# Attention, then a gated FFN, on one core: the kernel rewritten with hand-ordered engines

## The chip, the cores and the metric

One core of a Trainium2 chip runs the whole kernel. The metric is the device time of one execution in microseconds (us). Executions are called fast or slow by their time and by the clock that was granted to TensorE (PE below); ratios use fast ones only. DVE is VectorE, ACT is ScalarE, POOL is GpSimd, SP is SyncE, and PEld is TensorE's loading of weights. A line number such as L185 is a line of the profiled kernel. Numbers of before and of after are those of different programs, so the same line number means different things in them.

## The reference

Eight batches of 576 tokens, eight heads of 64. The attention is linear ("cosformer"): there is no softmax, only features, two small products and a division. Then comes a feed-forward network with a GELU gate, 512 to 1536 to 512, over all 4,608 tokens. All inputs and the output are fp32.

```python
def phi(x, c, s):                       # 64 -> 128 features
    r = np.maximum(x, 0.0)
    return np.concatenate([r * c, r * s], axis=-1)
q_p, k_p = phi(q, cos_w, sin_w), phi(k, cos_w, sin_w)
kv  = einsum('bhsf,bhsd->bhfd', k_p, v)
z   = sum(k_p, axis=2)
num = einsum('bhsf,bhfd->bhsd', q_p, kv)
den = einsum('bhsf,bhf->bhs', q_p, z)[..., None] + 1e-06
x   = (num / den), as tokens x 512
out = (gelu(x @ w_gate) * (x @ w_val)) @ w_out
```

In counts of 128x128x512 products, the FFN has 432 each for the gate, the value and the output. (The traces count 480 matmuls for the gate and 480 for the value, because some are narrower than 512.) That is nearly all the work of TensorE. The attention's products are small, but its transposes, scalings and loads are many.

## The kernel before

A scheduler orders the engines. The attention of a batch runs, then as many FFN chunks of 512 tokens as the finished batches allow. The parts that matter here:

```python
ffn_psum = ctx.enter_context(tc.tile_pool(name="ffn_psum", bufs=1, ...))   # one bank each: g_ps, v_ps, o_ps
def ffn_chunk(t0, n):
    for jt in range(JT):                       # 12 gate/value units
        g_ps = ...; for ct in range(CT): nc.tensor.matmul(g_ps[:, 0:n], lhsT=wg_sb[...], rhs=xT_sb[...])
        v_ps = ...; for ct in range(CT): nc.tensor.matmul(v_ps[:, 0:n], lhsT=wv_sb[...], rhs=xT_sb[...])
        nc.scalar.activation(gel[:, 0:n], g_ps[:, 0:n], AF.Gelu)
        nc.vector.tensor_mul(hT[:, jt, 0:n], gel[:, 0:n], v_ps[:, 0:n])
    ...                                        # o_ps: 12 matmuls per 128 tokens, copy, store
# loads: 256-byte rows, cast to bf16 on the GpSimd queue, one transfer per tile of 128 tokens
nc.gpsimd.dma_start(out=qk_sb[:L, 1], in_=q[b, :, ss:ss + L, :].transpose([1, 0, 2]))
# both transposes of the attention on TensorE, copied out by DVE and ACT
nc.tensor.transpose(out=qpt_ps[:, h, 0:L], in_=kqp[:L, 1, h, :], identity=ident[:L, :L])
nc.tensor.transpose(out=xt_view[:, 0:L], in_=attn_bt[:L, 4 * g:4 * g + 2, :], identity=ident[:L, :L])
```

## Time and profile before

Three runs before the prediction had a median of 412.06 us.

| | before |
|---|---|
| median of 3 runs | 412.06 us (410.91 to 413.91) |
| PE busy | 365.0 us, 89% of 411.5 us |
| one gate/value unit in the steady part | 1.87 us |
| one output tile (12 matmuls) | 2.59 us |
| last wo_sb in SBUF, its wait on the chain | 27.46 us |

From the page of the kernel before: busy time, two rows of the 40 slices (tenths busy; PEclk is the granted clock in tenths), the packets, and the chain of waits that ended last.

```profile
PE 365.0 (89%) x2467; PEld 192.7 (47%) x2512; DVE 181.0 (44%) x416; ACT 121.7 (30%) x256; POOL 102.8 (25%) x163
...
PE   0032899999999999999999999999999999999995
...
PEclk9999989999999999999999999999999999999999
...
DMA packets 121390, 29.90 MB, mean 73 GB/s; under 512 B 113168, under 2 KB 115728, under 8 KB 121360
...
PE 78%; DMA 10%; POOL 5%; DVE 3%; issue 2%; ACT 1%; DVEq 0%; POOLq 0%
PE v_ps L90 23%; PE o_ps L103 23%; PE g_ps L81 21%; DMA wo_sb<-in_moe_w_out_dram 7%; PE kv_ps L187 4%; PE qpt_ps L174 3%; DMA qk_sb<-in_k_dram 2%; DMA qk_sb<-in_q_dram 2%; PE nmA L203 2%; PE nmB L203 1%; DVE hT L99 1%; POOL qk_sb L129 1%; P
```

TensorE is full from the sixth slice on; the first four are nearly empty. So there are two parts: a start that waits for loads, and a long stretch in which only less TensorE time helps. Nearly all packets are under 512 bytes.

The timeline of TensorE in a stretch that holds FFN units only (start, duration, instruction, count; in other lines a bracket gives the idle time before the instruction and what ended it, where "issue" means nothing that the profile shows):

```profile
157.14 1.02 PE L90 MATMUL v_ps<-xT_sb,wv_sb 128*128 128x512 bf16 x4
158.00 1.03 PE L81 MATMUL g_ps<-xT_sb,wg_sb 128*128 128x512 bf16 x3
159.01 1.02 PE L90 MATMUL v_ps<-xT_sb,wv_sb 128*128 128x512 bf16 x4
```

The value products begin at 157.14 and 159.01: a unit takes 1.87 us. From value to gate it is 0.86 us, from gate to value 1.01 us. At 0.216 us for a matmul (2.59 / 12) eight would take 1.73 us. The timeline of weight loads has the missing 0.14 us: before each value group its second load waits 0.27 us. What it waits for the view of waits does not name ("issue"), but DVE's product of the unit before, which reads the one bank of v_ps, ends at 158.96 us, and the group begins at 159.01.

```profile
159.01 0.53 PEld L90 LDWEIGHTS <-wv_sb 128*128 128x128 bf16 x3 [0.27 <-issue]
```

### The profile page before, as it was taken

The page shows a single profiled execution, that of the slowest core. Times are in us where ns is not written, and L with a number is a line of the kernel's source. Part 1 is how long each engine was busy: PE and PEld are TensorE (multiplying, and loading weights), DVE is VectorE, ACT ScalarE, POOL GpSimd, SP SyncE. Part 2 cuts the span into 40 slices and gives each one's busy share as a digit, 9 for nine tenths or more (in the row PEclk, how much of TensorE's full clock was granted, in tenths as well). Part 3 has the DMA queues.
Part 4 walks back from the last instruction along what each step waited for, and adds up shares of the span by engine and source line. Part 5 has one row for each costly group of instructions (what it writes and reads, how often), then busy time and mean ns, then how long its engine had stood idle before and what let it go on. Part 6 is the DMA issues. An engine that isn't in the chain of part 4 may idle for free.

```text
span 411.5 us, 6371 instructions
## 1 busy us (share of the span) xinstructions
PE 365.0 (89%) x2467; PEld 192.7 (47%) x2512; DVE 181.0 (44%) x416; ACT 121.7 (30%) x256; POOL 102.8 (25%) x163
## 2 busy tenths in 40 slices
PE   0032899999999999999999999999999999999995
PEld 0031655554445553555455445644554444446672
DVE  0163658899232484239324832453245312312231
ACT  0100245252231252224323521343134323322231
POOL 9760578499900273012003100000000000000000
PEclk9999989999999999999999999999999999999999
DMA  9999999999971199119014601100110011011001
GB/s 155 156 169 208 208 160 127 85 103 173 186 46 51 54 103 72 52 51 60 0 53 69 41 2 52 53 0 2 51 53 2 0 51 53 0 51 53 27 26 52
DMA packets 121390, 29.90 MB, mean 73 GB/s; under 512 B 113168, under 2 KB 115728, under 8 KB 121360
## 3 DMA queue, kind: packets, MB, share of 16 engines
q0 software_dynamic: 106800, 17.70, 60.2%
q10 hardware_dynamic: 9872, 10.62, 8.2%
q1 hardware_dynamic: 4688, 1.18, 1.9%
q8 instruction: 19, 0.31, 0.3%
q14 instruction: 11, 0.09, 0.1%
HBM read 37.75 MB, written 9.44 MB: 115 GB/s over the span
## 4 chain that ended last, share of the span: by engine, by line
PE 78%; DMA 10%; POOL 5%; DVE 3%; issue 2%; ACT 1%; DVEq 0%; POOLq 0%
PE v_ps L90 23%; PE o_ps L103 23%; PE g_ps L81 21%; DMA wo_sb<-in_moe_w_out_dram 7%; PE kv_ps L187 4%; PE qpt_ps L174 3%; DMA qk_sb<-in_k_dram 2%; DMA qk_sb<-in_q_dram 2%; PE nmA L203 2%; PE nmB L203 1%; DVE hT L99 1%; POOL qk_sb L129 1%; POOL vx L142 1%; POOL qk_sb L136 1%; DVE kqp L166 1%
## 5 line engine op out<-in xcount | busy, mean ns | idle before, releaser
L99 DVE TENSOR_TENSOR hT<-gel,v_ps 128x512 bf16<-128x512 f32 (+1 forms) x120 | 75.8, 632 | 124.5 <-PE v_ps L90 112.5
L90 PE MATMUL v_ps<-xT_sb,wv_sb 128*128 128x512 bf16 (+1 forms) x471 | 116.4, 356 | 1.7 <-DVE hT L99 0.9
L81 PE MATMUL g_ps<-xT_sb,wg_sb 128*128 128x512 bf16 (+1 forms) x460 | 116.5, 358 | 1.1 <-issue 0.4
L103 PE MATMUL o_ps<-wo_sb,hT 128*128 128x512 bf16 x416 | 101.5, 379 | 2.2 <-ACT o_sb L111 0.7
L98 ACT ACTIVATE gel<-g_ps 128x512 f32<-128x512 f32 (+1 forms) x120 | 66.6, 555 | 115.7 <-PE g_ps L81 109.0
L90 PEld LDWEIGHTS <-wv_sb 128*128 128x128 bf16 x480 | 45.1, 97 | 49.8 <-issue 18.4
L103 PEld LDWEIGHTS <-hT 128*128 128x128 bf16 x432 | 41.3, 97 | 46.7 <-issue 1.7
L81 PEld LDWEIGHTS <-wg_sb 128*128 128x128 bf16 x480 | 44.5, 98 | 37.4 <-issue 1.4
L187 PE MATMUL kv_ps<-vx,kqp 128*128 128x65 bf16 (+1 forms) x320 | 28.0, 202 | 31.9 <-DVE kqp L162 21.9
L179 DVE COPY qpt_sb<-qpt_ps 128x1024 bf16<-128x1024 bf16 (+1 forms) x40 | 25.3, 633 | 55.4 <-PE qpt_ps L174 55.2
L111 ACT COPY o_sb<-o_ps 128x512 f32<-128x512 f32 x36 | 21.1, 585 | 90.7 <-PE o_ps L103 84.8
L187 PEld LDWEIGHTS <-kqp 128*128 128x128 bf16 (+1 forms) x320 | 19.9, 100 | 39.2 <-DVE kqp L162 21.9
L118 POOL MEMSET vx<- 128x8 bf16 (+1 forms) x40 | 7.0, 205 | 111.9 <-PE kv_ps L187 111.9
L136 POOL DMA_DIRECT2D qk_sb<-in_k_dram x35 | 31.5, 900 | 4.9 <-DVE kqp L166 2.4
L139 POOL DMA_DIRECT2D qk_sb<-in_q_dram x35 | 31.1, 889 | 3.2 <-DMA wo_sb<-in_moe_w_out_dram 1.9
L142 POOL DMA_DIRECT2D vx<-in_v_dram x35 | 30.4, 875 | 3.8 <-POOL vx L118 1.6
L174 PE MATMUL qpt_ps<-ident,kqp 128*128 128x128 bf16 (+1 forms) x320 | 27.2, 232 | 4.0 <-DVE qpt_sb L179 2.7
L174 PEld LDWEIGHTS <-kqp 128*128 128x128 bf16 (+1 forms) x320 | 21.7, 106 | 13.2 <-issue 4.3
L203 PEld LDWEIGHTS <-qpt_sb 128*128 128x128 bf16 (+1 forms) x320 | 18.5, 102 | 12.0 <-issue 7.2
L162 DVE TENSOR_SCALAR kqp<-qk_sb,cos_col 128x1024 bf16<-128x1024 bf16 (+3 forms) x40 | 21.7, 543 | 2.4 <-PE kv_ps L187 2.4
L166 DVE TENSOR_SCALAR kqp<-qk_sb,sin_col 128x1024 bf16<-128x1024 bf16 (+3 forms) x40 | 21.6, 540 | 0.0
L194 ACT CAST kv_sb<-kv_ps 128x260 bf16<-128x260 f32 x16 | 6.0, 375 | 41.2 <-PE kv_ps L187 40.4
(34 smaller groups left out, 172.5 us busy)
## 6 DMA issues: line engine op xcount, KB each, us to landing
out_dram<-o_sb ACTq DMA_DIRECT2D x36, 256.0 KB, 2.0
qk_sb<-in_q_dram POOLq DMA_DIRECT2D x32, 128.0 KB, 6.1
qk_sb<-in_k_dram POOLq DMA_DIRECT2D x28, 128.0 KB, 5.9
vx<-in_v_dram POOLq DMA_DIRECT2D x28, 128.0 KB, 5.7
wo_sb<-in_moe_w_out_dram POOLq DMA_DIRECT2D x1, 1536.0 KB, 27.5
wg_sb<-in_moe_w_gate_dram POOLq DMA_DIRECT2D x1, 1152.0 KB, 15.5
wv_sb<-in_moe_w_val_dram POOLq DMA_DIRECT2D x1, 1152.0 KB, 19.7
kf<-in_k_dram SPq DMA_DIRECT2D x4, 256.0 KB, 6.5
```

The source lines that it names most:

```text
L81: nc.tensor.matmul(g_ps[:, 0:n], lhsT=wg_sb[:, ct, jt * 128:(jt + 1) * 128], rhs=xT_sb[:, ct, t0:t0 + n], start=(ct == 0), stop=(ct == CT ...
L90: nc.tensor.matmul(v_ps[:, 0:n], lhsT=wv_sb[:, ct, jt * 128:(jt + 1) * 128], rhs=xT_sb[:, ct, t0:t0 + n], start=(ct == 0), stop=(ct == CT ...
L98: nc.scalar.activation(gel[:, 0:n], g_ps[:, 0:n], AF.Gelu)
L99: nc.vector.tensor_mul(hT[:, jt, 0:n], gel[:, 0:n], v_ps[:, 0:n])
L103: nc.tensor.matmul(o_ps, lhsT=hT[:, jt, tt * 128:(tt + 1) * 128], rhs=wo_sb[:, jt, :], start=(jt == 0), stop=(jt == JT - 1),)
L136: nc.gpsimd.dma_start(out=qk_sb[:L, 0], in_=k[b, :, ss:ss + L, :].transpose([1, 0, 2]))
L139: nc.gpsimd.dma_start(out=qk_sb[:L, 1], in_=q[b, :, ss:ss + L, :].transpose([1, 0, 2]))
L142: nc.gpsimd.dma_start(out=vx[:L, :, 0:D], in_=v[b, :, ss:ss + L, :].transpose([1, 0, 2]))
L166: nc.vector.tensor_scalar(dst_ap[..., D:F], src_ap, sin_col[:L, st:st + 1], 0.0, op0=ALU.mult, op1=ALU.max,)
L174: nc.tensor.transpose(out=qpt_ps[:, h, 0:L], in_=kqp[:L, 1, h, :], identity=ident[:L, :L],)
L187: nc.tensor.matmul(kv_ps[:, hh, :], lhsT=kp_tiles[st][:L, h, :], rhs=vx_tiles[st][:L, h, :], start=(st == 0), stop=(st == NST - 1),)
L203: nc.tensor.matmul(nm_ps[h // 4][:L, h % 4, :], lhsT=qpt_sb[:, h, 0:L], rhs=kv_sb[:, h, :], start=True, stop=True,)
```

## The change

The intent: take the attention's transposes off TensorE, give each product two PSUM banks, bring the data in sooner, and weave the small work of the attention between the FFN's units so that TensorE never waits. Every engine's order is written by hand. The first FFN block is 576 wide (256 and 320), the rest 512, the last 448, so that block n needs batches up to n only. The core of the diff:

```diff
-    ffn_psum = ctx.enter_context(tc.tile_pool(name="ffn_psum", bufs=1, space=bass.MemoryType.PSUM))
+    ps = pp.tile([128, 8, 512], FP32, name="ps")
...
+            gv_unit(n, jt, 0, w, jt % 2, 2 + jt % 2)            # two gate banks, two value banks
...
+    def src_main(t, b, h0, h1):                                 # 1 KB rows: partition p holds tokens 4p to 4p+3
+        return t[b, h0:h1, 0:MAIN, :].rearrange("h (p j) d -> p h (j d)", j=NJ)
+    def load_main(dst, t, b, h0=0, h1=H):                       # fp32, SyncE's queue
+        nc.sync.dma_start(out=dst[:, h0:h1].rearrange("p h j d -> p h (j d)"), in_=src_main(t, b, h0, h1))
...
+    def turn_q(b):
+        nc.sync.dma_start_transpose(out=qT[b % 2][:, 0:NJ]..., in_=qp[:, 0:NJ]...)
...
+        xb = rot.tile([128, 2, 4, D], BF16, name="xb", bufs=3)  # one normalised tile of the attention
+    def turn_x(b, t, xb):
+        nc.sync.dma_start_transpose(out=xT[:, :, p0:p0 + L], in_=xb[:L].rearrange("p g h d -> p (g h d)"))
...
+        a[s].append(L(prep_q, b, 0, 3))                         # after unit s of block n: work for batch b = n + 1
+        a[s + 1].append(L(prep_q, b, 3, 5))
+        a[s + 1].append(L(turn_q, b))
+        a[s + 1].append(L(prep_k, b, 0, 2))
+        a[s + 2].append(L(prep_k, b, 2, 5))
+        a[s + 2].append(L(prep_v, b))
+        if b + 1 < B:
+            a[s + 3].append(L(load_all, b + 1))                 # six loads, 3.5 MB
+        for i in range(6):
+            a[s + 3 + i].append(L(attn_step, b, i))             # kv, then five numerators, each with its turn_x
```

(In block 1 the loads of batch 2 come after unit 0 and s is 3; s is 0 from block 2 on.) Loads, stores and transposes all go through SyncE, in this order. Only the weights are loaded by GpSimd.

## The prediction

> **What bounds the kernel now.** TensorE. The page gives PE 365.0 us busy, 89% of 411.5 us; the slices show it at 9 from about 62 us to the end, and the chain of waits is 78% PE (v_ps, o_ps, g_ps 23, 23, 21%) plus 10% DMA, all early. Two parts: a start of about 60 us that waits for loads (wo_sb alone 27.5 us to landing, kv_ps waits 21.9 us for the first kqp), then about 350 us of full PE. In the steady part the timeline shows one gate/value unit (eight 128x512 matmuls) every 1.87 us, while twelve o_ps matmuls take 2.59 us, 0.216 us each. Eight at that pace would be 1.73 us: v_ps has one buffer, so its first weight load waits for the DVE product (0.27 us "issue", about 0.14 us lost).
>
> **What the change does to PE.**
> - Two g banks and two v banks: 0.14 us x 108 units = about 15 us saved.
> - Attention costs PE about 11 us per batch now. DMA takes both transposes for seven batches. What is left per batch: 40 kv_ps matmuls at 0.072 us pitch and 40 numerators at 0.033 us, 4.3 us. About 45 us saved over seven batches.
> - Start: 1 KB fp32 rows on the hardware queue instead of 256-byte cast rows on GpSimd (113,168 of 121,390 packets are under 512 B). q, k, v of batch 0 (3.5 MB) should be in by about 13 us, the first FFN matmul at about 23 us instead of about 55 us. Weights (9.4 MB read, at the about 400 GB/s of source that before reached) then arrive just ahead of the 1.96 us units of block 0.
>
> Sum (estimate): gate/value 96 x 1.73 + block 0 12 x 1.96 = 189; o_ps 36 x 2.59 = 93; attention 7 x 4.3 = 30; start 23; tail (copy, store) 3: 338 us if PE never waits.
>
> **What it adds.** DVE prepares fp32 q, k, v in program order: 20 scalings at 0.40 us pitch, casts about 2 us: 10 us per batch, with numerators 5 us and hT 12 x 0.65 us: about 23 us of a 36 us block, but bunched in three units. By hand, k and v are ready about 1.5 us after PE wants kv_ps, so 1 to 3 us of stall in each of six blocks; in block 0 (units 6 to 11) DVE has about 14 us for 12 us of PE: 4 to 6 us. Batch 1's attention, between blocks 0 and 1: 2 to 4. SP issues loads, stores and transposes in order. [...] Together about 16 us of stall.
>
> **Predicted: 354 us, 8 in 10 between 340 and 380.** Faster by over 2%: 0.93; within 2%: 0.03; slower: 0.04.
>
> **What would show it.** v_ps no longer waiting for hT; units at 1.73 us; PE busy near 315 us; first gate matmul at 20 to 26 us; longest PE waits behind DVE scalings at the third and fourth unit of blocks 1 to 6; q transposes landing in under 10 us; the last two blocks free of gaps.
>
> **What would make it wrong.** Transposing DMAs of 10 us or more, which hold the SP queue and with it stores, loads and xT; weights arriving slower[...]; DVE scalings of the strided fp32 rows slower than 0.40 us.

Two passages are cut from the recorded text and marked there: a bandwidth for transposing DMAs that no trace of this case shows, with the time and the slack reckoned from it, and a reason for slower weights that no run tested. Neither was a term of the sum. The 338 us without waits and the 16 us of stall still make the predicted 354, for the author took the q transposes to be quick enough to add no stall. The 400 GB/s of source are an estimate: twice the 208 GB/s that the page of the kernel before shows in its fourth and fifth slices, since the cast halves what arrives (a 128x512 tile of v loads as 256 KB in fp32 and as 128 KB in bf16 there). The text lets the first weight load wait for DVE; the timeline above shows the wait at the second. How long a transpose holds SyncE's queue only the later traces show: the issue of a large q transpose took 4.97 us in the median in the kernel after, and 5.2 us, 17.3 at most, in the slow run of e4.

## The result, and the profile after

All ratios here are the mean time of a kernel's fast runs over the mean of the fast runs of the kernel before in the same rounds, so they are not quite the ratio of the medians quoted beside them.

| | before | after |
|---|---|---|
| median | 412.99 us (410.91 to 415.15, 4 runs) | 384.18 us (383.68 to 386.0, 4 runs) |
| ratio | | 0.9309, 95% interval 0.9265 to 0.9353 |
| PE busy (profiled run) | 365.0 us | 327.6 us |
| granted clock (profiled run) | 0.996 | 0.945 |

It is faster, but 30 us above the prediction and outside its range. The page of the kernel after, the same rows:

```profile
PE 327.6 (85%) x2083; PEld 167.8 (44%) x2117; DVE 195.7 (51%) x431; ACT 104.2 (27%) x187; POOL 17.1 (4%) x30
...
PE   4678988793939896999599969996999999999995
...
PEclk9589999996979998999899998999999999999999
...
DMA packets 98954, 55.21 MB, mean 144 GB/s; under 512 B 64112, under 2 KB 94320, under 8 KB 98928
...
PE 60%; DVE 23%; DMA 12%; issue 3%; ACT 1%; DVEq 0%; POOL 0%; POOLq 0%; ACTq 0%
PE ps L214 19%; PE ps L223 18%; PE ps L249 16%; DMA xT<-xb 10%; DVE kp L137 7%; DVE qp L137 6%; DVE hT L227 3%; PE ps L185 3%; PE ps L168 3%; DMA qT<-qp 2%; DVE xb L197 2%; DVE vx L145 2%; DVE vx L121 1%; PE ps L277 1%; DVE qT L278 1%
```

TensorE is at 8 from the fourth slice (29 us) on. But its row has a dip in each block up to the slice that ends at 269 us (3 and 3 in block 1, then 6, 5, 6, 6), and the clock dips beside most of them. The chain went from 78% PE to 60%, and it has a new member: the transposing DMA of x, 10%.

What TensorE waited for, from the view of waits (total us, times, longest us):

```profile
PE ps L185 <- DVE xb L197: 20.5, 7, 4.2
PE ps L277 <- DVE qp L137: 7.8, 4, 4.0
PE ps L168 <- DVE vx L145: 6.3, 5, 5.4
PE ps L168 <- DVE vx L151: 3.8, 7, 0.7
```

L185 is the numerator of the attention. It waits for DVE's normalised tile xb to leave its PSUM bank. Five of the seven waits, one in each of blocks 1 to 5, make 18.0 us (4.16, 3.46, 3.98, 3.36, 3.06). Block 6 has none, and it is the one with attention but no loads. DVE itself waits:

```profile
DVE xb L197 <- DMA xT<-xb: 20.4, 5, 4.5
```

So DVE may not write a fourth xb before the DMA has turned the first: there are three buffers. One block shows why the turn is late. DVE's timeline of the block at 194 to 234 us:

```profile
212.92 0.69 DVE L197 TENSOR_TENSOR xb<-ps,rec 128x512 bf16<-128x512 f32 x1
...
217.08 0.69 DVE L197 TENSOR_TENSOR xb<-ps,rec 128x512 bf16<-128x512 f32 x1
...
219.47 0.69 DVE L197 TENSOR_TENSOR xb<-ps,rec 128x512 bf16<-128x512 f32 x1
...
227.50 0.69 DVE L197 TENSOR_TENSOR xb<-ps,rec 128x512 bf16<-128x512 f32 x1 [3.90 <-DMA xT<-xb]
```

SyncE's timeline of the same time (duration here is the time that its sequencer spent on the issue):

```profile
210.29 0.58 SPq L85 DMA_DIRECT2D qf<-in_q_dram  x1
...
212.39 3.40 SPq L90 DMA_DIRECT2D kr<-in_k_dram  x1
...
217.31 4.13 SPq L90 DMA_DIRECT2D vr<-in_v_dram  x1
221.53 2.11 SPq L205 DMA_TRANSPOSE xT<-xb  x1
```

The first tile was ready at 213.6, its turn was issued at 221.53, behind six loads whose issue took 11 us, and it landed 5.9 us later, beside them. Only then could DVE go on, and TensorE after it:

```profile
223.86 1.03 PE L223 MATMUL ps<-xT,wv_sb 128*128 128x512 bf16 x4
228.25 0.41 PE L185 MATMUL ps<-kv,qT 128*128 128x65 bf16 x8 [3.36 <-DVE xb L197]
...
230.82 1.92 PE L214 MATMUL ps<-xT,wg_sb 128*128 128x512 bf16 x4
...
233.64 1.03 PE L214 MATMUL ps<-xT,wg_sb 128*128 128x512 bf16 x4
```

A group of four that takes 1.03 us from start to end took 1.92 us after the stop. The table by windows (stretch, its length, busy time of the engines; the third number from the end is the granted clock) gives 0.50 from 230.2 to 231.8 and 1.00 from 233.4 on:

```profile
230.20:231.80 1.60, 1.60 (x5) 0.58 (x4) 0.66 (x1) 0.00 (x0) 0.00 (x0) 0.50 0.55 111
...
233.40:235.00 1.60, 1.60 (x9) 0.75 (x8) 0.69 (x1) 0.30 (x1) 0.00 (x0) 1.00 0.00 0
```

The stop was 3.36 us here and 3.06 us in block 5 (before 267.91 us), and both were followed by windows of clock 0.50 (in block 5 from 268.2 to 269.8 us). In e2, below, two shorter waits close together, of 2.36 and 0.66 us before 202.17 and 203.10 us, were followed by a group of four that took 1.75 us. These lengths come from traces in which the ends of matmuls are modelled, and no run here isolates how long a stop has to be.

### The profile page after: what moved, and what is told of

Same layout as the page of the kernel before. It is cut to its first block, busy times and chain, and to the rows that moved or that the text cites. A ratio compares the mean times of both kernels' runs of the same rounds, so it can differ in the third digit from the quotient of the medians.

```text
span 384.2 us, 5503 instructions
## 1 busy us (share of the span) xinstructions
PE 327.6 (85%) x2083; PEld 167.8 (44%) x2117; DVE 195.7 (51%) x431; ACT 104.2 (27%) x187; POOL 17.1 (4%) x30
## 2 busy tenths in 40 slices
DMA packets 98954, 55.21 MB, mean 144 GB/s; under 512 B 64112, under 2 KB 94320, under 8 KB 98928
## 3 DMA queue, kind: packets, MB, share of 16 engines
q1 hardware_dynamic: 93136, 50.15, 57.1%
q0 software_dynamic: 5792, 4.72, 7.8%
## 4 chain that ended last, share of the span: by engine, by line
PE 60%; DVE 23%; DMA 12%; issue 3%; ACT 1%; DVEq 0%; POOL 0%; POOLq 0%; ACTq 0%
PE ps L214 19%; PE ps L223 18%; PE ps L249 16%; DMA xT<-xb 10%; DVE kp L137 7%; DVE qp L137 6%; DVE hT L227 3%; PE ps L185 3%; PE ps L168 3%; DMA qT<-qp 2%; DVE xb L197 2%; DVE vx L145 2%; DVE vx L121 1%; PE ps L277 1%; DVE qT L278 1%
## 5 line engine op out<-in xcount | busy, mean ns | idle before, releaser
L227 DVE TENSOR_TENSOR hT<-gel,ps 128x512 bf16<-128x512 f32 (+3 forms) x120 | 75.2, 630 | 110.1 <-PE ps L223 98.0
L214 PE MATMUL ps<-xT,wg_sb 128*128 128x512 bf16 (+3 forms) x468 | 117.5, 370 | 5.9 <-DMA xT<-xb 3.5
L223 PE MATMUL ps<-xT,wv_sb 128*128 128x512 bf16 (+3 forms) x473 | 115.1, 366 | 2.4 <-DVE hT L227 2.3
L219 ACT ACTIVATE gel<-ps 128x512 f32<-128x512 f32 (+3 forms) x120 | 66.5, 554 | 141.6 <-PE ps L214 137.8
L249 PE MATMUL ps<-wo_sb,hT 128*128 128x512 bf16 x419 | 96.7, 379 | 0.4
L214 PEld LDWEIGHTS <-wg_sb 128*128 128x128 bf16 x480 | 45.4, 100 | 45.9 <-issue 10.1
L254 ACT COPY o_sb<-ps 128x512 f32<-128x512 f32 x36 | 21.1, 585 | 101.4 <-PE ps L249 87.1
L197 DVE TENSOR_TENSOR xb<-ps,rec 128x512 bf16<-128x512 f32 (+1 forms) x40 | 27.6, 689 | 21.6 <-DMA xT<-xb 20.4
L185 PE MATMUL ps<-kv,qT 128*128 128x65 bf16 x320 | 17.1, 196 | 21.6 <-DVE xb L197 20.5
L185 PEld LDWEIGHTS <-qT 128*128 128x128 bf16 x320 | 15.3, 99 | 31.0 <-issue 22.5
L168 PE MATMUL ps<-vx,kp 128*128 128x65 bf16 x320 | 13.5, 201 | 10.3 <-DVE vx L145 6.3
L168 PEld LDWEIGHTS <-kp 128*128 128x128 bf16 x320 | 12.6, 102 | 14.1 <-issue 11.1
L137 DVE TENSOR_SCALAR qp<-qf,cos_c 128x512 bf16<-128x512 f32 x32 | 15.2, 474 | 0.0
L137 DVE TENSOR_SCALAR kp<-kf,sin_c 128x512 bf16<-128x512 f32 x29 | 13.7, 472 | 0.0
L137 DVE TENSOR_SCALAR qp<-qf,sin_c 128x512 bf16<-128x512 f32 x28 | 13.4, 477 | 0.0
```

Of the source, the lines that this page charges most:

```text
L137: nc.vector.tensor_scalar(d, src, col[:L, j:j + 1], 0.0, op0=ALU.mult, op1=ALU.max)
L168: nc.tensor.matmul(ps[:, bank, (h % 4) * (D + 1):(h % 4 + 1) * (D + 1)], lhsT=kp[:, j, h, :], rhs=vx[b % 2][:, j, h, 0:D + 1], start=(j == ...
L185: nc.tensor.matmul(ps[:, bank + h // 4, (h % 4) * (D + 1):(h % 4 + 1) * (D + 1)], lhsT=qT[b % 2][:, t, h, :], rhs=kv[b % 2][:, h, 0:D + 1] ...
L197: nc.vector.tensor_tensor(xb[:L], nd[:, :, :, 0:D], rec[:L, :, :, None].to_broadcast([L, 2, 4, D]), op=ALU.mult)
L214: nc.tensor.matmul(ps[:, gb, 0:w], lhsT=wg_sb[:, ct, jt * 128:(jt + 1) * 128], rhs=xT[:, ct, p0:p0 + w], start=(ct == 0), stop=(ct == CT - 1),
L219: nc.scalar.activation(gel[:, 0:w], ps[:, gb, 0:w], AF.Gelu)
```

## The experiments

The theory after the first look: x is turned too late because SyncE issues the loads first, three xb buffers are too few to bridge it, and the stops cost their own length and a spell at half clock. Rivals: the loads slow down the transposes that run beside them, whatever the order of issue; the clock costs a lot by itself; or the stops hide other limits (DVE's preparation of q, k and v) and removing them gains little.

In the expected texts of e4 and e6 a clause is cut that had loads and transposes share the DMA engines; no trace here shows on which engine a packet ran.

All twelve kernels gave correct results. The chips differed, so each ratio is to the kernel before on the same chip; its median was 412.65 to 414.06 us. Multiplied by 413 us, the ratios are compared in us below ("by the ratios").

| run | median us | ratio to before |
|---|---|---|
| after | 384.18 | 0.9309 |
| e1_xb8 | 363.18 | 0.8779 |
| e2_loads_last | 376.97 | 0.9104 |
| e3_fill | 379.51 | 0.9174 |
| e4_loads_pool | 424.77 (one fast run: 414.4) | none |
| e5_start (on e1) | 359.21 | 0.8700 |
| e6_pool_gated | 401.42 | 0.9721 |
| e7_x_by_pe | 364.86 | 0.8832 |
| e8_prep2 (on e1) | 357.68 | 0.8678 |
| e9_one_v (on e1) | 369.24 | 0.8948 |
| e10_rows256 (on e1) | 393.67 | 0.9533 |
| e11_pool_gated_xb8 (on e1) | 379.98 (fast runs: 376.1) | 0.9111 |
| best (e1, e5 and e8) | 356.06 | 0.8622 |

### e1_xb8: eight buffers for the normalised tile

```diff
-        xb = rot.tile([128, 2, 4, D], BF16, name="xb", bufs=3)
+        xb = rot.tile([128, 2, 4, D], BF16, name="xb", bufs=8)
```

> Only the number of xb buffers goes from 3 to 8. Theory (order of issue): turn_x waits on SP behind six loads, so three xb buffers run out and DVE, then TensorE, stops in blocks 1 to 5 (18.0 us of PE waits for xb, plus about 10 us of half clock after them). With 8 buffers these waits go: 360 us, range 354 to 366; the first transpose of each batch is still issued some 8 us late. Rival A (DVE bunching costs the time): no change, 384. Rival B (xT itself late): the waits move to the gate matmuls of the next block, 375 to 384.

Measured: 363.18 us (362.42 to 365.32), as expected; by the ratios 21.9 us less than after. The waits of TensorE in its profile:

```profile
PE ps L214 <- DMA xT<-xb: 6.0, 3, 4.3
...
PE ps L185 <- DVE xb L197: 2.5, 2, 1.3
```

The waits for xb fell from 20.5 to 2.5 us, exactly the five stops, and the mean clock rose from 0.945 to 0.984. POOL's copies that close the blocks now stand 34.76 us apart in blocks 4 to 6 (after: 40.0 and 39.2 us in blocks 4 and 5, 34.75 in block 6); these two close blocks 4 and 5 in e1:

```profile
217.44 0.83 POOL L232 COPY hT<-hT 128x768 bf16<-128x768 bf16 x1 [33.94 <-DVE hT L227]
252.20 0.83 POOL L232 COPY hT<-hT 128x768 bf16<-128x768 bf16 x1 [33.93 <-DVE hT L227]
```

The transposes are no quicker (3.0 us median to landing, up to 7.8, against 2.5 and 7.3): the late turn remains, it only stopped nobody. One changed digit gives back 22 of the 30 us that were missing.

### e2_loads_last: the loads after the five x transposes, three buffers

```diff
-        if b + 1 < B:
-            a[s + 3].append(L(load_all, b + 1))
         for i in range(6):
             a[s + 3 + i].append(L(attn_step, b, i))
+        if b + 1 < B:
+            a[s + 8].append(L(load_all, b + 1))
```

> load_all of the next batch is issued after the five turn_x instead of before them; xb stays at 3. Theory (order of issue): xb waits go as with 8 buffers, but q arrives later, so the scalings of the next block start up to 5 us late and part comes back before kv: 362 to 374 us. Rival A (DVE bunching): worse than 384. Rival C (transposes are slow in themselves, whatever stands before them): transposes still land 6 us or more after issue and xb waits stay, 384.

Measured: 376.97 us, 3 us above the expected range. The stops went, as the theory says, but the loads were late for the next block:

```profile
PE ps L168 <- DVE vx L145: 15.3, 6, 5.7
...
PE ps L185 <- DVE xb L197: 2.5, 2, 1.3
```

L168 is the product of k and v. It waits 15.3 us for the cast of v, against 6.3 after. So the order of issue does set who waits, but the block has no place in which 3.5 MB of loads disturb nothing: early they hold up x, late they are late themselves. That is why the buffers, and not the order, are the repair.

### e3_fill: products that nobody needs, in place of the stops

```diff
         else:
+            if i == 5 and 2 <= b < B - 1:
+                dummies(14, 4)
             turn_x(b, i - 1, numer(b, i - 1, 6))
```

> Fourteen junk matmuls (3.0 us) on TensorE just before the numerator that waits for xb in blocks 1 to 5; nothing waits less. It splits the loss into wait and clock: if the half clock after each stop is a cost of its own, as the 1.5 to 1.9 us for four matmuls after the stops suggest, 2 us x 5 = 8 to 12 us come back, 372 to 376 us, and the granted clock of blocks 2 to 5 goes from 0.90 to 0.96 to 0.99. If the waits alone cost the time: 384 to 386.

Measured: 379.51 us, mean clock 0.984. By the ratios 5.6 us came back, less than the 8 to 12 us that the expected time asked for. The clock is back to that of e1, while DVE's wait for the x transposes is still 21.3 us. So of the 21.9 us of e1 about 5 are the half clock after the stops, and the rest is the stops themselves (18.0 us). The two add up to 23.6, nearly 2 us too many, so the 5.6 is no sharper than that.

### e4_loads_pool and e6_pool_gated: another queue for the loads

In e4 the six loads are issued by GpSimd, so that SyncE is free for the transposes. In e6 they moreover wait on GpSimd until the q transposes of the batch before have landed (one element is read). Both have three buffers.

```diff
     def load_all(b):
+        nc.gpsimd.tensor_copy(tiny[0:1, 0:1], qT[(b - 1) % 2][0:1, NJ, H - 1, REM - 1:REM])    # e6 only
-        load_main(qf, q, b)
+        load_main(qf, q, b, q=nc.gpsimd)
...                                              # likewise for the other five
```

> The loads of batches 2 to 7 go out on the idle GpSimd queue, at the same place in the program; xb stays at 3. Theory (order of issue on SP): turn_x is issued within 1 us of its xb and the xb waits shrink to under 1 us a block: 358 to 366 us. Rival (contention[...]): turn_x is issued early but lands 6 to 10 us later, the xb waits stay at 2 to 4 us, 378 to 386 us.

> The loads on GpSimd's queue again (424.8 us ungated), xb stays at 3, but before each set of loads GpSimd reads one element of the transposed q of the batch before, so loads start only when that transpose has landed. Theory (in the ungated run the loads overtook the q transposes[...], 43.5 us of waits for qT): qT waits fall under 5 us in total, 362 to 376 us. Rival (loads from GpSimd's queue hurt whatever they meet, or are slow themselves): waits move to the x transposes or the scalings, 385 us or more.

e4 took 424.77 us; its profiled run and two more were slow ones (clock 0.905 to 0.923), but its one fast run, 414.4 us, is also 30 us over after. The waits of the profiled, slow run:

```profile
PE ps L185 <- DMA qT<-qp: 43.5, 5, 22.7
PE ps L185 <- DVE xb L197: 11.8, 4, 6.7
```

The x transposes no longer stand behind loads (before the first one of block 3, issued at 208.18 us, SyncE has only a store and the q transposes; the 35 x transposes landed in 2.4 us in the median, 13.4 at most), but nothing keeps the loads behind the q transposes any more. Those landed after 13.4 us in the median and 30.2 at most, against 5.6 and 8.5 after. (Each batch has a large and a small one; the large ones alone have a median of 7.2 us in the kernel after.) The order that looked like the fault had been protecting the q transposes. Both of the written forecasts were wrong.

e6 restores that protection: q lands in 5.5 us again. It took 401.42 us, still 17 us worse than after, in fast runs only. From its view of DMA issues (count, median us from issue to landing) and of waits:

```profile
xT<-xb SPq DMA_TRANSPOSE x35, 8.9
```

```profile
PE ps L185 <- DVE xb L197: 21.7, 5, 8.0
PE ps L223 <- DVE hT L227: 12.9, 7, 4.3
```

The x transposes, issued promptly, run beside the loads and need 8.9 us, up to 14.6, where they needed 2.5. While DVE waits for a buffer (38.4 us in all) it can't make hT either, so the FFN's own units stop too (the 12.9 us above). The theory that the order of issue alone is the cause falls here, and what is seen fits the rival: beside loads a transpose takes longer, also when the loads are on another queue, 8.9 against 2.5 us for x and 13.4 against 5.6 us for q (the latter in e4's slow run). By what mechanism is not shown. e6 changes the kind of the loads' queue too (the profile lists 25.96 MB as software_dynamic, against 4.72 MB after, and 28.91 MB in place of 50.15 as hardware_dynamic), so it can't tell whether GpSimd's queue disturbs more than SyncE's. But the kernel after, where all is on SyncE's queue, shows the delay as well: its five x transposes of block 6, which has no loads, land in 2.3 to 2.5 us, and the first one behind the loads in 5.9 us in block 4 and 7.3 us in block 5. So in the block shown above the first turn was late twice: issued 7.9 us after its tile was ready, and then about 3.4 us slower than without loads.

### e11_pool_gated_xb8: the same placement with eight buffers

Its edit is that of e6 on e1.

> Base: the version with eight xb buffers (363.2 us) with its loads of batches 2 to 7 on the GpSimd queue, held until the q transposes of the batch before have landed. With three xb buffers this placement took 401.4 us, because the x transposes landed beside the loads, 8.9 us each. If the three buffers are the only way in which slow transposes reach TensorE: waits for xb under 4 us in all and 363 to 370 us. If slow transposes reach it by another way too (xT comes too late for the next block's first gate matmul, or the prepared q, k, v come late): 380 us or more, with waits for xT or for the copies of kv.

Two runs were fast (376.1 us both) and two slow (383.8 and 386.2); the ratio of the fast ones is 0.9111. So the eight buffers give back 25 us of e6's time, and the result still lies 13.7 us above e1 by the ratios, between the two ranges that were written down. The profile is of a slow run. It shows 2.5 us of waits for xb, and this:

```profile
PE ps L214 <- DMA xT<-xb: 22.3, 5, 8.6
```

L214 is the first gate product of a block, and it waits for the last x of the batch. With e1 that wait was 6.0 us. The eight buffers are therefore not the only way in which slow transposes reach TensorE: x must also be there when the next block begins. How much of the 13.7 us this is in a fast run has no profile, and stays open.

### e7_x_by_pe: x of batches 2 to 7 turned on TensorE, three buffers

```diff
+            if i > 1:
+                x_by_pe(i - 2, held.pop(), 5 if i <= 3 else 4, "s", b)
+            if i <= 5:
+                held.append(numer(b, i - 1, 6))
```

> Undoes one part of the change: for batches 2 to 7 the attention rows are turned on TensorE and copied by ScalarE; xb stays at 3, loads stay before. Theory (xb is held by x transposes queued behind loads): the xb waits are gone without more buffers; 30 tiles of four transposes cost TensorE about 0.3 us each, 9 us: 366 to 374 us, so still below 384 but above 363. If turning x by DMA were a gain as built, this would be 390 or more.

Measured: 364.86 us, a little better than expected. One of blocks 4 to 6 takes 35.98 us against 34.76 in e1, so the transposes cost TensorE 1.2 us a batch. Turning x by DMA was meant to save that. With three buffers it cost 19.7 us more than it saved (384.18 against 364.86, by the ratios); with eight it gains 2.2 us, which is not clear of the noise, since the intervals of e7 (0.8798 to 0.8867) and e1 (0.8735 to 0.8824) overlap.

### e5_start and e8_prep2: the two other places where TensorE waits, on e1

The start. DVE's timeline after, and then in e5, up to the first q copy:

```profile
2.27 2.26 DVE L121 MEMSET vx<- 128x2640 bf16 x1 [0.49 <-issue]
...
5.79 2.26 DVE L121 MEMSET vx<- 128x2640 bf16 x1 [0.50 <-issue]
...
10.29 0.69 DVE L278 COPY qT<-ps 128x1024 bf16<-128x1024 bf16 x1 [1.20 <-PE ps L277]
```

```profile
6.10 1.67 DVE L137 TENSOR_SCALAR qp<-qf,cos_c 128x512 bf16<-128x512 f32 x4 [2.62 <-DMA qf<-in_q_dram]
7.69 2.48 DVE L279 COPY qT<-ps 128x1024 bf16<-128x1024 bf16 x4
```

After, DVE first fills two whole tiles with ones, though only one column of each head needs it, and then in each of four rounds waits 1.2 us for TensorE's transposes before it may scale the next part. e5 removes both:

```diff
-        nc.vector.memset(vx[i], 1.0)
+        nc.vector.memset(vx[i][:, :, :, D:D + 2], 1.0)
...
         scale(qp, qf, qr, j, 1, "s")
+    for j in range(NJ):
         qb = ps[:, j % 4, :].bitcast(BF16)
```

> On the kernel with 8 xb buffers (363.2 us): only the ones column of vx is set, and all four q scalings stand before the four copies of qT on DVE. Theory (the late start is DVE program order: 5 us of memsets and 1.2 us of idle before each copy): the first gate matmul comes at 21 to 23 us instead of 27, the total is 357 to 359 us. Rival (first weights bound the start; they land at 18 to 20 us, later ones at 30 us): the gain is eaten in block 0, 361 to 364 us.

Measured: 359.21 us, first gate product at 22.90 us (after: 27.21), as expected, and the total 0.2 us above the expected range; 3.3 us by the ratios, whose intervals just overlap (0.8654 to 0.8746, e1 0.8735 to 0.8824).

In block 1, k times v waits 5.4 us at once for DVE: the loads of batch 2 are issued only in that block, so all of batch 2's preparation lies bunched in three units. e8 loads q and k of batch 2 before block 0's output tiles, and scales q between those:

```diff
+    load_main(qf, q, 2)
+    load_rem(qr, q, 2)
+    load_main(kf, k, 2)
+    load_rem(kr, k, 2)
     for i, m in enumerate(tiles0):
...
+            prep_q(2, 3 * (i - 1), 3 if i == 1 else 5)
...
+    turn_q(2)
+    load_main(vf, v, 2)
+    load_rem(vr, v, 2)
```

> On the kernel with 8 xb buffers (363.2 us): q and k of batch 2 are loaded before the four output tiles of block 0 and q is scaled between them, so that the scalings no longer bunch in block 1. Theory (block 1 and the first part of block 2 lose 5.4 us to the kv wait, 4.3 us to a late xT and some 3 us of half clock): 353 to 358 us. Rival (the loads now stand before the x transposes of batch 1 and delay block 1 by as much): 361 to 366 us.

Measured: 357.68 us, as expected; 4.2 us by the ratios. Block 1 ends at 107.35 us (e1: 106.04), block 2 at 142.16 (e1: 146.93): the gain appears a block later than I had thought.

### e9_one_v: one value bank, as before

```diff
-            gv_unit(n, jt, 0, w, jt % 2, 2 + jt % 2)
+            gv_unit(n, jt, 0, w, jt % 2, 2)
```

> Base: the version with eight xb buffers (363.2 us). Edit: the gate/value units of blocks 1 to 8 write their value product always to PSUM bank 2, as in the kernel before; the gate product keeps two banks. Theory (the second value bank is what took the unit from 1.87 to 1.73 us): units at about 1.87 us again, PE waits of 0.1 to 0.15 us for the DVE product in each of 96 units, 374 to 378 us. Rival (the unit got shorter for another reason, or DVE now runs far enough ahead that one bank would do): within 3 us of 363.

Measured: 369.24 us; 7.0 us over e1 by the ratios, between the two. Where two units follow each other directly, the old picture is back (two lines of its timelines, of TensorE, then of weight loads):

```profile
311.49 1.03 PE L214 MATMUL ps<-xT,wg_sb 128*128 128x512 bf16 x4
312.50 1.02 PE L223 MATMUL ps<-xT,wv_sb 128*128 128x512 bf16 x4
```

```profile
312.50 0.53 PEld L223 LDWEIGHTS <-wv_sb 128*128 128x128 bf16 x3 [0.27 <-issue]
```

The 1.01 us from gate to value and the 0.27 us at the second weight load are those of the kernel before. So the bank is the cause of the longer unit. But most units of the new kernel have an output tile or attention between them, which give DVE its time anyway: blocks 4 to 6 are only 0.44 us longer each (35.20 against 34.76). So the weaving seems to remove much of the same wait, and the bank alone is worth half of what I had given it. (Of the 8.3 us between the two profiled runs, 3.3 lie in block 2, 44.20 us against 40.89; why is not shown.)

### e10_rows256: rows of 256 bytes in place of 1 KB

```diff
-        return t[b, h0:h1, 0:MAIN, :].rearrange("h (p j) d -> p h (j d)", j=NJ)
+        return t[b, :, 128 * h0:128 * h1, :].rearrange("h p d -> p h d")
...
+        for j in range(h0 // 2, h1 // 2):
+            nc.sync.dma_start(out=dst[:, :, j, :], in_=src_main(t, b, j, j + 1))
```

> Base: the version with eight xb buffers (363.2 us). Edit: each partition again takes tokens 128 apart, so q, k and v are loaded in rows of 256 bytes, four transfers a tensor in place of one; still fp32 and still on the SyncE queue. Theory (1 KB rows are what makes the loads short): packets of 256 bytes rise above 100,000, batch 0 is in some 5 to 10 us later, the loads of one later batch last about twice as long, and the time rises to 372 to 395 us. Rival (the gain at the start came from spreading over queues and engines, and rows do not matter): within 3 us of 363.

Measured: 393.67 us, 31 us over e1, at the top of what was expected. Packets under 512 bytes rose from 64,112 to 163,520; the first gate product came at 33.32 us (e1: 27.24); TensorE waited 23.9 us for x at the starts of blocks. Why is not shown: this edit makes the rows shorter and also issues four transfers where there was one, and SyncE's issuing is 9% of its chain, so the rows and the issues are not told apart.

### best: the three repairs together

> Three repairs together: eight xb buffers, the start put right (only the ones columns of vx are set; all four q scalings ahead of the copies), and q and k of batch 2 loaded and q scaled before block 1. Alone over the version with eight buffers the last two gave 4.0 and 5.5 us. They touch different stages, so they should add: 363.2 - 4.0 - 5.5 = 353.7, 350 to 357 us. If block 1 was covering for the start (or the reverse), they do not add, and it stays at 357 to 360.

Measured: 356.06 us (353.16 to 357.7, 6 fast runs), ratio 0.8622, interval 0.8584 to 0.8659; it beats both kernels. By the ratios it is 6.5 us better than e1, where e5 and e8 alone make 7.4. That is within the expected range. The first gate product is at 24.22 us, not at the 22.90 of e5: ACT waited longer for v (its cast began at 14.86 us, in e5 at 13.54), so what remains of the start is the loads. Blocks 2 to 6 take 34.8 us each at a clock of 1.00.

## Why the prediction was right or wrong

**Right: what TensorE has to do.** A unit takes 1.73 us (0.86 and 0.86 in the timeline), output tiles 2.59 us, and the last two blocks are free of gaps, with block 7 at 31.08 us against a sum of 12 x 1.73 + 4 x 2.59 = 31.1. The attention costs a block 34.76 - 31.08 = 3.7 us of TensorE where 4.3 was predicted. The value product waits for hT only four times, 2.3 us in all.

**Right: the terms for DVE and the q transposes.** Scalings have a pitch of 0.40 us on the strided fp32 rows. k times v waits 0.3 us in block 2 and some 0.9 us in each of blocks 3 to 6 (predicted 1 to 3 in each of six blocks); only in block 1 the term was too small, with 5.9 us. The large q transposes landed in 7.2 us in the median, 8.5 at most; "under 10 us" held. The slack covered the measured time: TensorE's numerators waited for qT once, 0.9 us.

**Right by its total, wrong by its reason: the second value bank.** "0.14 us x 108 units = about 15 us saved" was 7 us when the bank alone was taken away (e9). The sum used 1.73 us a unit and did not suffer.

**Small slips of the sum.** It counted the last block as 512 wide, it is 448: 12 x 1.73 / 8 = 2.6 us too many, so the time without waits is about 335.4 and not 338. The first gate product came at 27.2 and not at 23 us. That was not the loads but DVE's order of work: e5 brought it to 22.9. PE busy was 327.6, not 315, in part because busy time grows at half clock (a group of four took 1.92 us in place of 1.03; best, at a mean clock of 0.977 against 0.945, has 318.2).

**Wrong, the step that failed: "Together about 16 us of stall".** It was 384.2 - 335.4 = 49 us. The runs divide it so, by the ratios:

| part of the stall | us | shown by |
|---|---|---|
| stops for xb with the half clock after them | 21.9 | e1 (18.0 us of stops; about 5 of clock, e3) |
| batch 2 bunched in block 1 | 4.2 | e8 |
| DVE's order at the start | 3.3 | e5 |
| remaining | 20.7 | best: 356.1 - 335.4 |

(The lines sum to 50, since e5 and e8 together gave 1 us less than the sum of the two.)

What remains is near the 16 us that were predicted; nearly all of it lies in the first 104 us, since blocks 2 to 7 of best have no gaps to speak of. The error is the first line. The prediction wrote "SP issues loads, stores and transposes in order" and then followed that sentence for the q transposes only. It named as the danger that slow transposes would hold the loads. It was the other way round. The loads held the x transposes, which are small and come right after them in the program, and a pool of three buffers passed the delay on: DMA to DVE (20.4 us of waits), DVE by way of its PSUM bank to TensorE (20.5 us), and TensorE to its own clock (0.945 in the mean, 0.984 in e1). The numerators had one pair of PSUM banks throughout; whether a second pair would have helped was not tried. All of that could be read in the diff: `load_all` stands one line above the steps that turn x, and `bufs=3` in a batch of five tiles.

**What stayed open.** How much of e10's 31 us is the row size and how much the fourfold issues. Where e11's last 13.7 us went in a fast run. And what a shorter start would need now that it waits for v's load.

## What to carry to other kernels

For each rotating buffer ask what frees it, on which queue that stands, and behind what; a buffer freed by a DMA needs enough copies for the longest burst ahead of that DMA. Here, with five tiles a batch, three were too few (20.5 us of waits) and eight were enough (2.5 us). The time on the issuing queue counts in such a burst: loads of 128 KB took 3.40 and 4.13 us to issue in the kernel after, one took 7.56 us in best, and a large q transpose 4.97 us. Before moving loads to another queue to speed things up, ask what the old order was protecting: in e4 the q transposes landed after 13.4 us in place of 5.6, in e6 those of x after 8.9 us in place of 2.5, though the loads were on another queue. A stop of TensorE can cost more than its length (here 18.0 us of stops cost 21.9 us, the half clock included), so one that comes back in each block is worth finding even when the shares of busy time look good.
